# Attention, expert layer and second layer on one core: thresholds in pairs, v and the exchange at other steps

## Chip, cores, metric

One core of a Trainium2 chip. The time is the device time of one execution in microseconds (us). The engines are named as the profile names them: PE (TensorE, products), DVE (VectorE), ACT (ScalarE), POOL (GpSimd), SP (SyncE, which here issues nearly all DMAs).

## What is computed

Attention with a threshold near each row's maximum, then a layer of eight experts of which each token uses one, then a second layer. All inputs are 32-bit floats; the change touches the attention alone.

```python
batch, n_heads, seq, head_dim = (4, 8, 576, 64)
def _attn_ref(q, k, v, tau):
    scale = 1.0 / np.sqrt(q.shape[-1])
    scores = scale * np.matmul(q, k.transpose(0, 1, 3, 2))
    thresh = np.max(scores, axis=-1, keepdims=True) - tau
    scores = np.where(scores >= thresh, scores, -1000000000.0)
    scores = scores - np.max(scores, axis=-1, keepdims=True)
    attn = np.exp(scores)
    attn = attn / (np.sum(attn, axis=-1, keepdims=True) + 1e-09)
    return np.matmul(attn, v)

def reference(q, k, v, tau, moe_*, moe2_*):
    attn_out = _attn_ref(q, k, v, tau)
    x = attn_out.transpose(0, 2, 1, 3).reshape(B * S, H * D)
    x = _moe_ref(x=x, **moe)      # 2304 tokens, one of 8 experts each
    return _moe2_ref(x=x, **moe2) # (h - tanh(h)) @ w_out
```

## The kernel before

The attention runs as 16 units, numbered 0 to 15; a unit is one head of two batch entries. A unit has nine steps, t = 0 to 8, of 128 query rows against 576 keys, so that there are 144 steps in one row, numbered i = 9u + t. Whatever else a unit needs (loads, splitting and transposing q and k, the exchange, the weights of v, P times V, logits) is put at a step relative to the unit's first one, and at a phase 0 to 3 of that step, by the table `PL`; `PFIRST` and `PLAST` override it for the first and the last unit. `run` walks through the steps and issues: phase 0, the scores of step i+2 on PE, phase 1, the maximum of step i+1 on DVE (`smax`, L234) and its exponential on ACT (`sexp`, L240), the mask of step i on DVE (`smask`, L253, which multiplies the exponential by "score at or above the threshold" and sums the row), the threshold of step i+1 on DVE (`sthr`, L244), then phases 2 and 3. That order is the order in which each engine executes: every engine and SP's queue work strictly in order, and the waits between them are semaphores that the framework derives from who writes and reads what.

Score tiles lie in PSUM in three buffers of two banks each (`asp`), so the scores of step i+2 need the buffer that the mask of step i-1 frees. One more bank, tile `ops`, holds in disjoint columns two halves of P times V (`self.ops`, products L297, read by `pv_out`, L303), the logits (`self.lm`, products L557, read at L564 and L566) and the v sums (`self.vsum`, product L130, read at L135). The last bank, tag "t", is a single buffer through which pass the transposes of q and k (`tr`, L167), the exchange products (`turn`, L204) and the transposes for the logits (L549).

The exchange of a unit makes a copy of q with its two halves of partitions swapped: three products with a flip matrix (`s0`, `s1`, `s2`, L204), each copied out by DVE (`x0`, `x1`, `x2`, L209). After it come the transposes of k in two parts (`k0`, `k5`, L167), each copied out by ACT (`ek0`, `ek5`, L193). They are placed five to seven steps ahead of the unit that needs them, that is in steps t = 2 to 5 of the unit before.

v is loaded for four units at a time by six DMAs from SP (`lv`, L106 and L108). Each of the four units has a maximum of |v| on DVE (`vm`, L126), then once for the four a sum on PE (`vn`) and three small operations on DVE (`vc`, L135 to L137) make a scale. The first four units have places of their own in `PFIRST`; the others, beginning at units 4, 8 and 12, take theirs from `PL`. The weights after the mask go through a cast on ACT (L261), a subtraction on POOL (L265) and a DMA transpose that SP issues (`te`, L272), three per unit, each for three of its P times V groups, seven steps later.

All that follows the attention (experts, second layer) stays as it is.

Of the kernel before, what the change touches and what calls it, by code (L numbers as in the profile page):

```python
# [11 lines left out]
F32 = mybir.dt.float32  # L12
# [6 lines left out]
ALU = mybir.AluOpType  # L19
# [11 lines left out]
class Attn:  # L31
# [3 lines left out]
    def __init__(self, tc, ctx, q, k, v, tau, xtok, ident):  # L35
        self.tc, self.nc = tc, tc.nc
        self.q, self.k, self.v = q, k, v
        self.xtok, self.ident = xtok, ident
        nc = self.nc
        e = ctx.enter_context  # L40
        self.one = e(tc.tile_pool(name="a1", bufs=1))
        self.ld = e(tc.tile_pool(name="ald", bufs=2))
        self.wk = e(tc.tile_pool(name="awk", bufs=2))
        self.sp = e(tc.tile_pool(name="asp", bufs=3, space=PSUM))
        self.tp = e(tc.tile_pool(name="atp", bufs=1, space=PSUM))
        one = self.one
        self.raw, self.x2, self.vv, self.vs, self.vh, self.ka = {}, {}, {}, {}, {}, {}
        self.X, self.rr, self.rqk, self.tpu = {}, {}, {}, {}
        w = one.tile([128, 1], F32, name="warm")
        nc.vector.memset(w, 0.0)  # L50
        nc.scalar.activation(out=w, in_=w, func=AF.Exp)
        t = one.tile([128, 1], F32, name="tau")
        nc.gpsimd.dma_start(out=t, in_=tau.to_broadcast([128, 1]))
        self.load_qk(0, 0, 0, 1, nc.sync)
        self.load_qk(0, 1, 0, 1, nc.scalar)
        self.identr = one.tile([128, 128], F32R, name="identr")
        nc.vector.tensor_copy(self.identr, ident)
        self.flip = one.tile([128, 128], F32R, name="flip")
        for o in (0, 64):
            nc.vector.tensor_copy(self.flip[:, o:o + 64], ident[:, 64 - o:128 - o])  # L60
        self.g8 = one.tile([128, 1], F32, name="g8")
        nc.vector.tensor_scalar(out=self.g8, in0=t, scalar1=0.0, scalar2=0.125, op0=ALU.is_ge, op1=ALU.mult)
        self.ntau = one.tile([128, 1], F32, name="ntau")
        nc.vector.tensor_scalar(out=self.ntau, in0=t, scalar1=0.0, scalar2=-1.0, op0=ALU.max, op1=ALU.mult)
        z = one.tile([128, 64], F32, name="z64")
        nc.gpsimd.memset(z, 0.0)
        self.QA, self.QB = [], []
        for i in range(2):
            for lst, nm in ((self.QA, "qa"), (self.QB, "qb")):
                tl = one.tile([128, 2 * QS], F32R, name=f"{nm}{i}")  # L70
                nc.vector.tensor_copy(tl[:, S:S + 64], z)
                lst.append(tl)
        bank = self.tp.tile([128, 512], F32, name="ops")
        self.ops = bank[:, 0:6 * D].rearrange("p (a b d) -> p a b d", a=2, b=3)
        w = 6 * D + 9 * H
        self.lm = bank[:, 6 * D:w].rearrange("p (t e) -> p t e", t=9)
        self.vsum = bank[:, w:w + 4]
        self.c14 = one.tile([128, 128], F32, name="c14")
        nc.gpsimd.memset(self.c14, 2.0 ** -14)
        self.em, self.e16, self.et, self.sums = {}, {}, {}, {}  # L80
# [147 lines left out]
                i += 1  # L228
        return ps

    def smax(self, ps):
        nc = self.nc
        n = self.wk.tile([128, 2], F32, tag="n", name="n", bufs=6)
        nc.vector.tensor_reduce(out=n[:, 0:1], in_=ps[:, :, 0:288], axis=AX.XY, op=ALU.max, negate=True)  # L234
        return n

# [3 lines left out]
        nc.scalar.activation(out=e, in_=ps[:, :, 0:288], func=AF.Exp, bias=n[:, 0:1])  # L240
        return e

    def sthr(self, n):
        self.nc.vector.tensor_scalar(out=n[:, 1:2], in0=n[:, 0:1], scalar1=-1.0, scalar2=self.ntau, op0=ALU.mult, op1=ALU.add)  # L244

    def smask(self, u, t, ps, n, e):
        nc = self.nc
# [58 lines left out]
    def store(self, u):  # L306
        nc = self.nc
        P, h = divmod(u, H)
        if h % 2 == 1:
            c = slice((h - 1) * D, (h + 1) * D)  # L310
            X = self.X[u // 2]
            for j in range(2):
# [4 lines left out]

    LD = (6,)

    PL = {"lq": (-21, 1), "lk": (-31, 2), "lv": (-12, 1), "hi0": (-16, 2), "hi1": (-15, 3), "lo0": (-13, 1),  # L320
# [15 lines left out]

    AFTER = ["lq hi0", "lk hi1", "hi0 lo0", "hi1 lo1", "lo0 q0", "lo0 q4", "lo0 m", "lo1 m", "lo1 k0", "lo1 k5", "q0 eq0",
             "eq0 m", "m em", "em q4", "q4 eq4", "eq4 k0", "k0 ek0", "ek0 k5", "k5 ek5", "eq0 swap", "em swap", "eq4 swap", "vm vn", "vn vc", "vc vw", "vw vh", "vh vl", "se sl", "sl te", "po2 st",
             "po0 t0", "po1 t1", "po2 t2", "t0 v0", "v0 t1", "t1 v1", "v1 t2", "t2 v2", "v0 l0", "v1 l1", "v2 l2", "l0 la", "l1 la", "l2 la", "de rc", "em s0", "eq4 s0", "s0 x0", "x0 s1", "s1 x1", "x1 s2", "s2 x2"]

    def run(self, units, moe=None):
        nc = self.nc
        NU = len(units)
        sched = {}
        PL = self.PL
        for x in self.AFTER:
            x, y = x.split()
            assert PL[x] < PL[y] or PL[x] == PL[y] and list(PL).index(x) < list(PL).index(y), (x, y)

        def at(b, job, f, *a):  # L350
            i, ph = PL[job]
            sched.setdefault((b + i, ph), []).append((f, a))

        for n, u in enumerate(units):
            b = 9 * n
            PL = {**self.PL, **(self.PFIRST if n == 0 else self.PLAST if n == NU - 1 else {})}
            if n % 4 == 0:
# [46 lines left out]
        steps = [(u, t) for u in units for t in range(9)]  # L404
        ps, nn, ee = {}, {}, {}
        first, last = min(sched)[0], max(sched)[0]
        for i in range(first, last + 1):
            if i == 4 and moe:
                moe.consts()
            for f, a in sched.get((i, 0), []):  # L410
                f(*a)
            if 0 <= i + 2 < len(steps):
                ps[i + 2] = self.scores(*steps[i + 2])
            for f, a in sched.get((i, 1), []):
                f(*a)
            if 0 <= i + 1 < len(steps):
                nn[i + 1] = self.smax(ps[i + 1])
                ee[i + 1] = self.sexp(ps[i + 1], nn[i + 1])
            if 0 <= i < len(steps):
                self.smask(*steps[i], ps.pop(i), nn.pop(i), ee.pop(i))  # L420
            if 0 <= i + 1 < len(steps):
                self.sthr(nn[i + 1])
            for ph in (2, 3):
                for f, a in sched.get((i, ph), []):
                    f(*a)
# [933 lines left out]
```

## Time and profile before

| | us |
|---|---|
| timed runs: median (lowest, highest of 3) | 1076.59 (1075.49, 1080.34) |
| profiled execution | 1076.63 |
| its span, first to last instruction | 1074.5 |
| busy: PE / DVE / ACT / POOL | 957.3 / 895.3 / 671.5 / 730.7 |
| first maximum L234 to last mask L253, starts | 15.2 to 332.1 |

The profile is one execution. A row of an instruction gives its start from the span's start, its duration, engine, line, operation, output and input, and in brackets how long the engine sat idle before it and which instruction released it. Durations of neighbours on DVE overlap by some 0.08 us in this profile, so that costs are read from start to start. The attention fills the first third of the span.

### The profile page before, as it was taken

How to read it: one execution, taken by the hardware profiler on the slowest of the kernel's cores; microseconds unless marked ns; L12 is line 12 of the kernel's file. 1: busy time of each engine (PE TensorE's matmuls, PEld its weight loads, DVE VectorE, ACT ScalarE, POOL GpSimd, SP SyncE). 2: the span in 40 equal slices, each digit the busy share in tenths (PEclk: the TensorE clock that was granted, in tenths of full speed). 3: DMA queues.
4: the chain of work that ended last, by engine and by line, in shares of the span. 5: the costliest groups of instructions: out<-in, count | busy, mean ns of one | idle time of the engine just before them, and what ended most of it. 6: DMA issues, size and time to landing. Idle time of an engine off the chain costs nothing.

```text
span 1074.5 us, 20770 instructions
## 1 busy us (share of the span) xinstructions
PE 957.3 (89%) x7342; PEld 876.6 (82%) x7342; DVE 895.3 (83%) x1635; ACT 671.5 (62%) x1262; POOL 730.7 (68%) x645
## 2 busy tenths in 40 slices
PE   4688897887787488999999988999999999999997
PEld 3576786776677387989999988888999999998986
DVE  5899888888884698977798876998989889888894
ACT  5797887986974154444455557666665666656662
POOL 3897887886874364455656567787867768677763
PEclk9698888898988599999999999999999999999999
DMA  6798999998989485877787976220101101000000
GB/s 160 145 213 165 211 205 152 225 202 163 175 155 169 149 292 199 278 227 247 258 290 252 295 247 177 76 76 20 40 8 38 30 20 40 8 31 1 20 11 30
DMA packets 247368, 153.16 MB, mean 143 GB/s; under 512 B 179642, under 2 KB 222028, under 8 KB 247261
## 3 DMA queue, kind: packets, MB, share of 16 engines
q1 hardware_dynamic: 243501, 141.02, 53.2%
q0 software_dynamic: 3312, 10.49, 2.8%
q8 instruction: 59, 0.97, 0.4%
q14 instruction: 48, 0.39, 0.1%
q10 hardware_dynamic: 448, 0.30, 0.1%
HBM read 85.08 MB, written 23.60 MB: 101 GB/s over the span
## 4 chain that ended last, share of the span: by engine, by line
PE 50%; DVE 9%; issue 3%; DMA 2%; ACT 1%; POOL 0%; another core or an unknown queue 0%; POOLq 0%; DVEq 0%; SPq 0%; ACTq 0%
PE h L1040 25%; PE y L1123 15%; PE y L1095 9%; DVE w L1236 2%; DVE w L1237 2%; PE t L1017 1%; DVE w L1234 1%; DMA xr<-rows,idx 1%; DVE cv L1157 1%; DVE tm L1235 1%; DVE w L1238 1%; DMA raw<-in_moe_w_dram 1%; DVE w L1010 1%; DMA raw<-wscr 0%; DVE cm L1159 0%
## 5 line engine op out<-in xcount | busy, mean ns | idle before, releaser
L265 POOL TENSOR_TENSOR e<-em,e 128x1024 f16<-128x1024 f32 (+1 forms) x98 | 158.1, 1613 | 55.0 <-ACT e L261 23.5
L1233 POOL TENSOR_SCALAR tm<-u 128x384 uint8<-128x384 f32 x88 | 129.7, 1474 | 51.4 <-ACT u L1229 50.8
L1040 PE MATMUL h<-xa,w 128*128 128x256 f32 (+6 forms) x864 | 140.5, 313 | 7.6 <-DVE hbuf L1076 6.8
L1095 PE MATMUL y<-hbuf,w 128*128 128x256 f32 (+6 forms) x864 | 139.5, 310 | 0.6 <-ACT yo L1098 0.6
L1040 PEld LDWEIGHTS h<-xa,w 128*128 128x128 f32 x864 | 130.5, 194 | 9.9 <-DVE hbuf L1076 8.1
L240 ACT ACTIVATE e<-sps,n 128x576 f32<-128x576 f32 x144 | 110.6, 768 | 34.8 <-DVE n L234 33.7
L1010 POOL TENSOR_TENSOR w<-raw,w 128x1024 fp32r<-128x1024 f32 x36 | 91.8, 2551 | 56.0 <-ACT w L1008 28.8
L1095 PEld LDWEIGHTS y<-hbuf,w 128*128 128x128 f32 x864 | 127.5, 191 | 1.3 <-ACT yo L1098 0.8
L1236 DVE SCALAR_TENSOR_TENSOR w<-y,w 128x384 f32<-128x384 f32 x96 | 123.3, 1284 | 0.0
L1229 ACT ACTIVATE u<-h 128x384 f32<-128x384 f32 x96 | 47.1, 491 | 117.3 <-PE h L1040 116.4
L253 DVE SCALAR_TENSOR_TENSOR em<-sps,n,e 128x576 f32<-128x576 f32 x144 | 116.6, 810 | 4.0 <-ACT e L240 2.4
L234 DVE TENSOR_REDUCE n<-sps 128x1 f32<-128x576 f32 x144 | 107.1, 744 | 12.3 <-PE sps L226 11.8
L1250 POOL TENSOR_TENSOR gl<-w,gh 128x384 fp32r<-128x384 f32 x83 | 85.7, 1032 | 38.0 <-ACT gh L1249 38.0
L1040 PE MATMUL h<-xk,w 128*128 128x384 f32 x576 | 109.6, 338 | 0.7 <-DVE w L1010 0.5
L297 PE MATMUL ops<-vh,et 128*128 128x64 f16 (+1 forms) x2240 | 97.4, 201 | 13.0 <-DVE x L303 12.1
L1040 PEld LDWEIGHTS h<-xk,w 128*128 128x128 f32 x576 | 102.1, 188 | 5.6 <-DVE w L1010 1.3
L297 PEld LDWEIGHTS <-et 128*128 128x128 f16 (+1 forms) x2240 | 83.6, 107 | 25.3 <-issue 21.1
L261 ACT CAST e<-em 128x576 f16<-128x576 f32 x144 | 99.9, 695 | 1.2 <-DVE em L253 1.2
L1075 ACT ACTIVATE hbuf<-h 128x256 fp32r<-128x256 f32 (+6 forms) x72 | 31.2, 433 | 108.3 <-PE h L1040 108.2
L226 PE MATMUL sps<-ka,qa 128*128 128x288 f32 x320 | 87.7, 367 | 9.4 <-DVE em L253 5.7
L1008 ACT CAST w<-raw 128x1024 fp32r<-128x1024 f32 x72 | 75.6, 1051 | 21.4 <-DVE free L597 11.6
L1123 PE MATMUL y<-w,gh 128*128 128x512 f32 x258 | 81.1, 395 | 3.2 <-POOL w L1010 1.5
(228 smaller groups left out, 2296.8 us busy)
## 6 DMA issues: line engine op xcount, KB each, us to landing
raw<-in_moe_w_dram SPq DMA_DIRECT2D x64, 512.0 KB, 5.2
cv<-in_moe_w_in_dram SPq DMA_DIRECT2D x16, 512.0 KB, 5.0
cv<-in_moe_w_out_dram SPq DMA_DIRECT2D x16, 512.0 KB, 5.4
wscr<-cm SPq DMA_DIRECT2D x32, 256.0 KB, 3.2
raw<-wscr SPq DMA_DIRECT2D x16, 512.0 KB, 3.8
xw<-yT SPq DMA_DIRECT2D x24, 192.0 KB, 2.7
vv<-in_v_dram SPq DMA_DIRECT2D x8, 512.0 KB, 5.1
raw<-in_q_dram SPq DMA_DIRECT2D x6, 576.0 KB, 7.7
```

The lines of the kernel that those rows point to most:

```text
L234: nc.vector.tensor_reduce(out=n[:, 0:1], in_=ps[:, :, 0:288], axis=AX.XY, op=ALU.max, negate=True)
L240: nc.scalar.activation(out=e, in_=ps[:, :, 0:288], func=AF.Exp, bias=n[:, 0:1])
L253: nc.vector.scalar_tensor_tensor(out=self.em[u, g][:, i].rearrange("p (a b) -> p a b", a=2), in0=ps[:, :, 0:288], scalar=n[:, 1:2], in1=e, ...
L261: self.nc.scalar.copy(self.e16[u, g][:, i, 0:S], self.em[u, g][:, i])
L265: eng.tensor_tensor(out=e16[:, r, S + 64:], in0=em[:, r, 0:512], in1=e16[:, r, 0:512], op=ALU.subtract)
L297: nc.tensor.matmul(o[q], lhsT=et[:, base + c, q], rhs=vh[:, a, j, c if c < 5 else c - 5, :], start=(n == 0), stop=(n == len(terms) - 1))
L1010: (self.nc.gpsimd if pool else self.nc.vector).tensor_tensor(out=l, in0=raw, in1=h.bitcast(F32), op=ALU.subtract)
L1040: self.nc.tensor.matmul(out, lhsT=a, rhs=b, start=(i == 0), stop=(i == len(parts) - 1))
L1095: nc.tensor.matmul(self.ys[d], lhsT=a[:, f % 2, s], rhs=b, start=(f == 0 and i == 0), stop=(f == 7 and i == 2))
L1123: nc.tensor.matmul(self.ys[m], lhsT=a[:, s], rhs=b[:, f % 2], start=(f == 0 and i == 0), stop=(f == 15 and i == 2))
L1233: nc.gpsimd.tensor_scalar(out=mk, in0=u, scalar1=RCUT * RCUT, scalar2=None, op0=ALU.is_gt)
L1236: V.scalar_tensor_tensor(out=w, in0=y, scalar=b, in1=w, op0=ALU.add, op1=ALU.mult)
```

## The change

Three things are done at once. (1) `smax` puts the negated maxima of two neighbouring steps into one tile of four words (maximum, threshold, maximum, threshold), and in every even step, right behind the maximum of step i+1 and its exponential, one subtraction makes both thresholds of the pair from -tau, which now stands twice in PSUM (`ntau2`, two columns of the bank `ops`). Odd steps issue none. (2) v is loaded at step -18 of its group instead of -12, its maxima come at -5 instead of -7, its sum and scale at -1 instead of -3. (3) The exchange copies `x0`, `x1`, `x2` come one or two phases later, the first k transposes move from phase 0 to phase 1 (behind the scores), their copy on ACT from phase 0 to phase 2, and the second k transposes from phase 2 to phase 3.

```diff
         self.vsum = bank[:, w:w + 4]
+        self.ntau2 = bank[:, w + 4:w + 6]
+        nc.vector.tensor_copy(self.ntau2, self.ntau.to_broadcast([128, 2]))
...
-    def smax(self, ps):
+    def smax(self, ps, i):
         nc = self.nc
-        n = self.wk.tile([128, 2], F32, tag="n", name="n", bufs=6)
+        if i % 2 == 0:
+            self.n2 = self.wk.tile([128, 2, 2], F32, tag="n", name="n", bufs=4)
+        n = self.n2[:, i % 2]
...
-    def sthr(self, n):
-        self.nc.vector.tensor_scalar(out=n[:, 1:2], in0=n[:, 0:1], scalar1=-1.0, scalar2=self.ntau, op0=ALU.mult, op1=ALU.add)
+    def sthr(self):
+        n = self.n2
+        self.nc.vector.tensor_tensor(out=n[:, :, 1], in0=self.ntau2, in1=n[:, :, 0], op=ALU.subtract)
...
-    PL = {"lq": (-21, 1), "lk": (-31, 2), "lv": (-12, 1), "hi0": (-16, 2), "hi1": (-15, 3), "lo0": (-13, 1),
+    PL = {"lq": (-21, 1), "lk": (-31, 2), "lv": (-18, 1), "hi0": (-16, 2), "hi1": (-15, 3), "lo0": (-13, 1),
...
-          "eq4": (-8, 0), "k0": (-5, 0), "ek0": (-5, 0), "k5": (-5, 2), "ek5": (-4, 0), "swap": (-8, 0),
-          "s0": (-7, 2), "x0": (-7, 3), "s1": (-6, 1), "x1": (-6, 2), "s2": (-6, 3), "x2": (-6, 3),
-          "vm": (-7, 3), "vn": (-3, 1), "vc": (-3, 2), "vw": (4, 3), "vh": (5, 3), "vl": (6, 1),
+          "eq4": (-8, 0), "k0": (-5, 1), "ek0": (-5, 2), "k5": (-5, 3), "ek5": (-4, 0), "swap": (-8, 0),
+          "s0": (-7, 2), "x0": (-6, 0), "s1": (-6, 1), "x1": (-6, 3), "s2": (-6, 3), "x2": (-5, 0),
+          "vm": (-5, 3), "vn": (-1, 1), "vc": (-1, 2), "vw": (4, 3), "vh": (5, 3), "vl": (6, 1),
...
             if 0 <= i + 1 < len(steps):
-                nn[i + 1] = self.smax(ps[i + 1])
+                nn[i + 1] = self.smax(ps[i + 1], i + 1)
                 ee[i + 1] = self.sexp(ps[i + 1], nn[i + 1])
+                if i % 2 == 0:
+                    self.sthr()
             if 0 <= i < len(steps):
                 self.smask(*steps[i], ps.pop(i), nn.pop(i), ee.pop(i))
-            if 0 <= i + 1 < len(steps):
-                self.sthr(nn[i + 1])
```

The list of what must come after what (`AFTER`) gains "x2 k0".

## Rows read from the trace of the kernel before

**Rows 1.** Windows: us; busy (x count) PE, PEld, DVE, ACT, POOL; PEclk; DMA; GB/s

```profile
80.00:335.00 255.00, 211.47 (x2749) 189.53 (x2750) 222.16 (x575) 211.61 (x370) 207.22 (x212) 0.89 0.99 183
```

**Rows 2.** Waits of DVE, 15 to 335: who <- whom: us in total, times, longest

```profile
DVE n L234 <- PE sps L226: 11.8, 17, 3.2
DVE qb L209 <- PE tws L204: 9.4, 18, 0.8
DVE pm L126 <- DMA vv<-in_v_dram: 9.3, 3, 5.3
DVE em L253 <- ACT e L240: 2.4, 11, 0.5
```

**Rows 3.** Timeline of DVE, a step without waits (start, duration, instruction)

```profile
258.67 0.75 DVE L234 TENSOR_REDUCE n<-sps 128x1 f32<-128x576 f32 x1
259.33 0.81 DVE L253 SCALAR_TENSOR_TENSOR em<-sps,n,e 128x576 f32<-128x576 f32 x1
...
260.07 0.21 DVE L244 TENSOR_SCALAR n<-n,ntau 128x1 f32<-128x1 f32 x1
260.19 0.74 DVE L234 TENSOR_REDUCE n<-sps 128x1 f32<-128x576 f32 x1
```

**Rows 4.** Groups by line (busy us, mean ns | idle before); L135 with ns min/median/max

```profile
L1157 DVE SCALAR_TENSOR_TENSOR cv<-cv,cm 128x512 uint32<-128x512 uint32 x32 | 41.7, 1303 | 1.1
L1237 DVE SCALAR_TENSOR_TENSOR w<-y,w 128x384 f32<-128x384 f32 x96 | 74.8, 780 | 10.4 <-DVE w L1236 0.5
...
L135 DVE TENSOR_SCALAR pm<-ops x4: 151/154/163, 38.5 to 256.2; 128x4 f32<-128x4 f32 x4
```

**Rows 5.** Timeline, two engines on interleaved words of one tile (cv)

```profile
396.74 0.43 DVE L1159 TENSOR_SCALAR cm<-cv 128x512 f32<-128x512 f32 x1
396.74 0.69 ACT L1163 ACTIVATE cv<-cv 128x512 f32<-128x512 f32 x1 [1.04 <-DVE cv L1157]
```

**Rows 6.** Timeline, logits read beside products in the same bank

```profile
148.18 1.00 PE L557 MATMUL ops<-wg,xT 128*128 128x8 f32 x4
...
149.57 0.97 PE L297 MATMUL ops<-vh,et 128*128 128x64 f16 x14
150.57 0.23 DVE L566 TENSOR_TENSOR L<-L,ops 128x72 f32<-128x72 f32 x1 [0.82 <-PE ops L297]
```

**Rows 7.** Timeline of DVE and PE, eighth step (t = 7) of unit 13

```profile
292.46 0.76 DVE L234 TENSOR_REDUCE n<-sps 128x1 f32<-128x576 f32 x1
...
295.29 0.76 DVE L234 TENSOR_REDUCE n<-sps 128x1 f32<-128x576 f32 x1 [0.64 <-PE sps L226]
...
293.55 0.97 PE L297 MATMUL ops<-vh,et 128*64 128x64 f16 x28
```

**Rows 8.** Timeline of DVE, SP and PE around the third load of v; landings of transposes

```profile
245.16 0.82 DVE L126 TENSOR_REDUCE pm<-vv 128x1 f32<-128x640 f32 x1 [5.34 <-DMA vv<-in_v_dram]
...
236.62 0.63 SPq L106 DMA_DIRECT2D vv<-in_v_dram  x1
...
224.83 4.07 SPq L272 DMA_TRANSPOSE et<-e  x1
...
234.53 0.58 PE L297 MATMUL ops<-vh,et 128*128 128x64 f16 x14
...
DMA to landing us min/median/max: 5.9/6.9/9.0
```

**Rows 9.** Timeline of PE and ACT, fifth step (t = 4) of unit 10

```profile
225.59 0.53 PE L167 MATMUL tps<-identr,x 128*128 128x128 f32 x4 [0.45 <-DVE qb L209]
...
226.16 0.59 ACT L193 CAST ka<-tps 128x512 fp32r<-128x512 f32 x1 [0.90 <-PE tps L167]
...
226.65 0.75 ACT L240 ACTIVATE e<-sps,n 128x576 f32<-128x576 f32 x1
...
227.43 0.67 ACT L261 CAST e<-em 128x576 f16<-128x576 f32 x1
...
227.93 0.51 PE L226 MATMUL sps<-ka,qa 128*128 128x288 f32 x2
```

More of the change, by code (lines that the diff above doesn't have):

```diff
@@ L338 @@
              "eq0 m", "m em", "em q4", "q4 eq4", "eq4 k0", "k0 ek0", "ek0 k5", "k5 ek5", "eq0 swap", "em swap", "eq4 swap", "vm vn", "vn vc", "vc vw", "vw vh", "vh vl", "se sl", "sl te", "po2 st",
-             "po0 t0", "po1 t1", "po2 t2", "t0 v0", "v0 t1", "t1 v1", "v1 t2", "t2 v2", "v0 l0", "v1 l1", "v2 l2", "l0 la", "l1 la", "l2 la", "de rc", "em s0", "eq4 s0", "s0 x0", "x0 s1", "s1 x1", "x1 s2", "s2 x2"]
+             "po0 t0", "po1 t1", "po2 t2", "t0 v0", "v0 t1", "t1 v1", "v1 t2", "t2 v2", "v0 l0", "v1 l1", "v2 l2", "l0 la", "l1 la", "l2 la", "de rc", "em s0", "eq4 s0", "s0 x0", "x0 s1", "s1 x1", "x1 s2", "s2 x2", "x2 k0"]
     def run(self, units, moe=None):
```

## Prediction, made before the change was timed

> **What bounds the kernel now.** The change touches the attention stage alone, some 330 of the 1074.5 us, so I read the stage first and not the page. The windows view [rows 1] shows VectorE (DVE) busy for 222.2 of the 255.0 us from 80 to 335, against 211.6 for ScalarE (ACT), 211.5 for TensorE (PE) and 207.2 for GpSimd: DVE is the fullest engine, but the other three are close behind, so an operation taken from DVE is not sure to shorten anything. PE also ran at a mean of 0.89 of its clock there, a mixture of 2.4 and 1.2 GHz. The waits of DVE [rows 2] say where its other time went: 11.8 us for scores, 9.4 us for the exchange products `tws`, 9.3 us in three waits for the DMA of v, the longest 5.3 us, and 2.4 us for the exponential.
>
> Where nothing holds DVE, a step is [rows 3]: maximum from 258.67, mask from 259.33, threshold from 260.07, next maximum from 260.19, 1.52 us in all. An instruction starts some 0.08 us before the one ahead has ended as long as it doesn't need its result: the mask starts 0.66 after the maximum, the threshold 0.74 after the mask, and the threshold, 0.21 long, delays the next maximum by 0.12 to 0.13. That 0.125, and not 0.21, is what one threshold costs. The order of before also keeps one instruction between each result and its reader.
>
> **A. One subtraction for two thresholds.** It removes 144 thresholds and adds 72. An odd step then has maximum and mask alone, 1.40 us, a gain of 72 x 0.125 = 9.0 us. In an even step the subtraction stands between the maximum it reads and the mask that reads it, and DVE has to wait for its own result twice. Two rows show what that costs [rows 4]: L1157, which reads what the instruction ahead wrote, has 1.1 us of idle time over 32, 34 ns each; L1237, which waits for DVE and for another engine as the mask does, has 10.4 us over 96, 108 ns each. The nearest row to the subtraction itself is L135, 4 elements out of PSUM in 154 ns. So an even step is 0.75 for the full maximum + 0.034 to 0.108 + 0.154 + 0.108 + 0.74 for the mask = 1.79 to 1.86, against 1.52: the 72 of them lose 19 to 24 us. Net, where DVE sets the pace throughout: +10 to +15 us. The cover is what DVE now waits for anyway, right behind the subtraction: the 2.4 us for exponentials goes; of the exchange waits, those in the third step of the six even units from 4 to 14 fall in an even step and take 0.3 each, 2 us; of the 11.8 us for scores, 8.6 come beside the longest, 3.2 at the start, and I let about half of them, 4 us, hide it. That leaves 12 - 8.5 = **+3.5 us**; the ends are -9 (every even step hidden) and +15 (none).
>
> The two maxima of a pair lie interleaved with their thresholds in one tile, and the exponential reads a maximum while the subtraction writes beside it. If that counted as a conflict each pair would wait for an exponential. The trace speaks against it [rows 5]: L1159 on DVE read the odd words of a tile from 396.74 on while L1163 on ACT wrote the even words of the same tile from 396.74 on.
>
> **B. tau in the PSUM bank of the products.** `ntau2` lies in the bank into which the P times V products (L297), the logits and the v sums are written. Such neighbours exclude each other [rows 6]: L566 reads the logits columns, whose last product L557 ended at 149.18, DVE was free at 149.76, yet it began only at 150.57, 0.82 later, when an L297 product into other columns of that bank had ended. So each subtraction waits for the P times V products issued before it, and those after it wait for the subtraction. Queued behind the waiting subtraction on DVE are the mask, and behind that the PSUM buffer that the next scores need. The price is read at the worst place, the eighth step of odd units [rows 7]: the maximum ended at 293.22, the products at 294.52, 1.30 later. The mask would then start at 294.52 + 0.04 + 0.154 + 0.108 = 294.82 and the next maximum at 295.56 instead of 295.29, since 0.64 of waiting for scores followed anyway: 0.27 net. There are seven odd units with such a step, 1.9 us; elsewhere the products mostly end just before the maximum, for which I add 1 us. B = **+3 us**; the ends are 0 and 7 x 1.30 = 9 us.
>
> The Trainium skill has a rule that speaks against this placement: "PSUM — Partial Sum Buffer", section "PSUM bank collisions raise a hardware error", says that two engines may not be in one bank (and quadrant of partitions) at the same time even at different addresses, so that software guards by bank and not by address. The 0.82 us of L566 agree with it; guarded by address alone, B would be nothing and the sum 3 us lower.
>
> **C. v loaded six steps earlier, its maximum two steps later.** The maximum of v (L126) [rows 8] waited 5.34 us for the load that SyncE (SP) issued from 236.62 on; the three such waits sum to 9.3 us [rows 2], and DVE, in order, held everything behind them. Six steps earlier the load lands over 10 us ahead: -9.3 us. Two things come back. First, the maxima no longer stand between the second exchange copy and the third, so three units get the waits for products that the others have, 9.4 us in 18 or 0.5 each [rows 2]: +1.5. Second, SP's queue is in order, and the six issues of v, at 0.63 and a little more each, 4.0 us, move in front of two transposes, the first issued at 224.83, and of four stores of X that nobody in the stage reads. The first transpose's product started at 234.53, 9.7 us after the issue, of which landing takes 5.9 to 9.0 (median 6.9): a slack of 0.7 to 3.8. Shifted by 4.0, it comes 0.2 to 3.3 us late, 1.2 at the median, of which I put down 1 us. The other two groups' transposes are issued somewhat longer ahead, and I take them to hold. C = -9.3 + 1.5 + 1 = **-7 us**, ends -9.3 and 0 (all three groups late by 2 to 3 us). One v sum and its three small DVE operations keep their distance from the maxima: nothing.
>
> **D. The exchange.** On DVE the three copies `x0` to `x2` keep their order among its instructions, because nothing of DVE's stands between the old place and the new: nothing. On PE the first k transposes (`k0`) go behind the scores, so the scores are no longer behind the 0.45 that `k0` waits for `x2` [rows 9]; 15 units x 0.45 = 6.8 us is the most this can give back. But on ACT their copy goes behind the exponential and the cast: 226.16 + 0.75 + 0.67 + 0.59 = 228.2 instead of 226.75. `k5` uses the same single PSUM tile and waits for that copy, and behind `k5` on PE are the next scores: 228.2 + 0.5 = 228.7 instead of 227.93, 0.8 late. Twelve units without v maxima (which cover it) x 0.8 = 9 us at most. DVE is slower by about 0.3 in the even step there, so a part is covered: **+3 us**, ends -7 and +9.
>
> **The sum.** 3.5 + 3 - 7 + 3 = +2.5 us of span; the copy that fills `ntau2` runs once before the first scores and counts nothing. The profiled execution took 1076.63 us, the median of the three timed runs is 1076.59, so the forecast is 1076.6 + 2.5 = 1079.1 us. A measurement of this kernel tells about 0.5%, 5.4 us, from no change.
>
> **The rivals.** (1) *The paired threshold is paid in full.* The place is the even step; the price is the two waits of DVE for itself, +12 to +15 instead of +3.5, with B at 3, C at -7 and D at +3: 1088 to 1091, on average 1089. For it: DVE is the fullest engine, and the waits for scores move with DVE, because a score tile starts when a mask frees its buffer. Against it: 2.4 + 9.4 + 11.8 us of waiting right behind. It turns the result slower than 1082 as soon as A costs over 6.4, that is, when less than half of the 12 is hidden. (2) *Only the v wait counts.* A and D vanish in existing waits, B nearly so: -9.3 + 1.5 + 0.5 gives 1069. For it: the 5.34 us are plain and lie on the fullest engine; against it: the gaps of [rows 4] and the bank of [rows 6]. (3) *The wait moves from v to the transposes.* SP's 4.0 us make the products late in all three groups, C goes to -1: 1085. For it: the 0.7 us of slack at the slowest landing; against it: the longer lead of the other two groups. (4) *The pair waits for the exponential after all*, 0.75 us [rows 9] x 72 = 54 more: 1133; against it, [rows 5].
>
> **How the numbers follow.** Forecast 0.39; (1) 0.20; (2) 0.27; (3) 0.13; (4) 0.01. Slower by over 0.5% are (1), (3) and (4), 0.34; faster (2), 0.27; same the forecast, 0.39. The likeliest is the forecast, 1079.1 us, by itself 1073 to 1082. Cases of either sign hold most of the chance, so the range takes in (2) with a little more of v's wait, 1067, and (1) to its end, 1091.
>
> **What would show it.** A: a pair of steps of 3.15 to 3.25 us against 3.05, with a gap ahead of the subtraction and of the mask. B: waits of the new subtraction for L297, about one per odd unit, near 1 us. C: no wait of L126 for the DMA; waits of L297 for a transpose near the end of units 2, 6 and 10. D: waits of the maximum for scores in the sixth and seventh step of most units. I am wrong if the subtraction costs far less than 0.3 us in its step, if the k copies on ACT don't hold PE up, or if the mask's wait for the exponential is what DVE's new gaps fall into everywhere.

## The result, and the profile after

| | us, median (lowest, highest) | runs | ratio to before [95%] |
|---|---|---|---|
| before, timed beside it | 1076.05 | 4 | 1 |
| changed | 1083.92 (1082.18, 1085.51) | 4 | 1.0067 [1.004, 1.0094] |

The change makes the kernel 7.2 us slower (0.0067 x 1076.05), a little beyond the 0.5% that can be told from no change. The time lies inside the range of the forecast, 1067 to 1091, but the forecast itself, 1079.1, was 4.8 us too low and on the other side of the 0.5%. Rival (3), 1085, came nearer. The profiled execution took 1085.51 us, its span is 1083.5 us.

The span grew by 9.0 us, and 6.3 of them lie between the first and the last mask (313.7 before, 320.0 after); the first mask starts 1.0 later. The windows view from the first mask to the last, in the kernel before and in the changed one (us; busy and count of PE, PEld, DVE, ACT, POOL, then PEclk, DMA, GB/s):

```profile
18.43:332.13 313.70, 256.31 (x3222) 227.83 (x3221) 276.76 (x723) 260.85 (x454) 254.32 (x294) 0.88 0.95 179
```

```profile
19.41:339.40 319.99, 259.75 (x3208) 228.68 (x3207) 274.07 (x649) 263.78 (x453) 254.25 (x294) 0.90 0.93 174
```

DVE has 2.7 us less work there, and TensorE's granted clock is not lower (0.90 against 0.88). The kernel became slower all the same, because DVE's idle time rose from 36.9 to 45.9 us. DVE's waits from 15 to 345 us, which takes in the longer stage, to be laid beside [rows 2] (in this kernel the maximum is L238, the exponential L244, the subtraction L249, the mask L258, the exchange copy L211, the products of P and V L302):

```profile
DVE n L238 <- PE sps L228: 17.7, 23, 3.9
DVE qb L211 <- PE tws L206: 8.2, 17, 0.9
DVE n L249 <- PE ops L302: 4.4, 6, 1.2
DVE em L258 <- ACT e L244: 3.1, 4, 1.8
```

The 9.3 us for v are gone, as foretold. In their place stand 5.9 more for scores and 4.4 for the products in the bank of `ntau2`; and the waits for exponentials, which the new gaps should have swallowed, are 3.1 in four, up to 1.8 each, where there were eleven of 0.5 at most. These four rows sum to 33.4 us, those of [rows 2] to 32.9, so they don't hold the 9.0 us of new idle time. The groups by line do (busy, mean ns, then all idle time just before them and the longer waits in it); first the mask before, then the mask and the subtraction after:

```profile
L253 DVE SCALAR_TENSOR_TENSOR em<-sps,n,e 128x576 f32<-128x576 f32 x144 | 116.6, 810 | 4.0 <-ACT e L240 2.4 <-issue 1.1 <-POOL x L122 0.3
```

```profile
L258 DVE SCALAR_TENSOR_TENSOR em<-sps,n,e 128x576 f32<-128x576 f32 x144 | 117.1, 813 | 11.9 <-ACT e L244 3.1 <-DVE n L249 0.5 <-ACT vv L142 0.5
...
L249 DVE TENSOR_TENSOR n<-ops,n 128x2 f32<-128x2 f32 x72 | 11.5, 160 | 10.4 <-PE ops L302 4.4
```

Take these waits off, and 0.2 us of short gaps are left before and 7.8 + 6.0 = 13.8 after. So the stretch changed by 13.6 of gaps, -2.7 of work and -4.6 for all waits taken together, which makes its 6.3 us. A pair of steps shows the gaps, in the timeline of DVE:

```profile
236.18 0.76 DVE L238 TENSOR_REDUCE n<-sps 128x1 f32<-128x576 f32 x1 [0.19 <-PE sps L228]
237.04 0.16 DVE L249 TENSOR_TENSOR n<-ops,n 128x2 f32<-128x2 f32 x1
237.33 0.82 DVE L258 SCALAR_TENSOR_TENSOR em<-sps,n,e 128x576 f32<-128x576 f32 x1
...
238.07 0.75 DVE L238 TENSOR_REDUCE n<-sps 128x1 f32<-128x576 f32 x1
...
239.48 0.75 DVE L238 TENSOR_REDUCE n<-sps 128x1 f32<-128x576 f32 x1
```

From maximum to maximum the even step takes 1.89 and the odd one 1.41; the even steps without a wait take 1.73 to 1.90, with 1.87 in the middle. The maximum ends at 236.94 and the subtraction starts at 237.04, that ends at 237.20 and the mask starts at 237.33: two gaps, 0.10 and 0.13 (0.10 in most steps), that [rows 4] had priced at 0.034 to 0.108.

### The profile page after: what moved, and what is told of

Its sections match the earlier page's. It is cut to its first block, busy times and chain, and to the rows that moved or that the text cites. A ratio compares the mean times of both kernels' runs of the same rounds, so it can differ in the third digit from the quotient of the medians.

```text
span 1083.5 us, 20711 instructions
## 1 busy us (share of the span) xinstructions
PE 962.9 (89%) x7342; PEld 879.9 (81%) x7342; DVE 892.1 (82%) x1564; ACT 675.0 (62%) x1262; POOL 731.4 (68%) x645
## 4 chain that ended last, share of the span: by engine, by line
PE 46%; DVE 11%; issue 3%; DMA 2%; ACT 2%; POOL 0%; another core or an unknown queue 0%; SPq 0%; POOLq 0%; DVEq 0%; ACTq 0%
PE h L1045 23%; PE y L1128 14%; PE y L1100 8%; DVE w L1242 2%; DVE w L1241 2%; DMA raw<-in_moe_w_dram 1%; DVE w L1239 1%; DVE cv L1162 1%; PE t L1022 1%; DVE w L1015 1%; DVE tm L1240 1%; DMA xr<-rows,idx 1%; ACT w L1013 1%; DVE w L1243 1%; DVE cm L1164 0%
## 5 line engine op out<-in xcount | busy, mean ns | idle before, releaser
L244 ACT ACTIVATE e<-sps,n 128x576 f32<-128x576 f32 x144 | 107.7, 748 | 46.9 <-DVE n L238 42.2
L258 DVE SCALAR_TENSOR_TENSOR em<-sps,n,e 128x576 f32<-128x576 f32 x144 | 117.1, 813 | 11.9 <-ACT e L244 3.1
L238 DVE TENSOR_REDUCE n<-sps 128x1 f32<-128x576 f32 x144 | 107.4, 746 | 17.8 <-PE sps L228 17.7
L1241 DVE SCALAR_TENSOR_TENSOR w<-y,w 128x384 f32<-128x384 f32 x96 | 121.7, 1268 | 0.0
L302 PEld LDWEIGHTS <-et 128*128 128x128 f16 (+1 forms) x2240 | 87.3, 108 | 29.5 <-issue 23.2
L302 PE MATMUL ops<-vh,et 128*128 128x64 f16 (+1 forms) x2240 | 97.4, 202 | 14.7 <-DVE x L308 7.6
L266 ACT CAST e<-em 128x576 f16<-128x576 f32 x144 | 96.6, 672 | 5.8 <-DMA et<-e 4.6
L1242 DVE SCALAR_TENSOR_TENSOR w<-y,w 128x384 f32<-128x384 f32 x96 | 79.5, 828 | 10.0
```

What stands on the lines that cost most here:

```text
L258: nc.vector.scalar_tensor_tensor(out=self.em[u, g][:, i].rearrange("p (a b) -> p a b", a=2), in0=ps[:, :, 0:288], scalar=n[:, 1:2], in1=e, ...
L302: nc.tensor.matmul(o[q], lhsT=et[:, base + c, q], rhs=vh[:, a, j, c if c < 5 else c - 5, :], start=(n == 0), stop=(n == len(terms) - 1))
L1241: V.scalar_tensor_tensor(out=w, in0=y, scalar=b, in1=w, op0=ALU.add, op1=ALU.mult)
L1242: V.scalar_tensor_tensor(out=w, in0=z, scalar=d, in1=w, op0=ALU.add, op1=ALU.mult)
```

## The experiments

Every kernel is the one before with some edit, or the changed one with an edit undone, timed in five rounds against the kernel before on the same chip. "Stretch" is first to last mask in the profiled execution (313.7 before, 320.0 changed). The kernels were timed on three chips, on which the kernel before took 1077.3, 1080.1 and 1077.7 us, so that kernels are compared by their ratios; in brackets is the 95% interval.

| kernel | edit | median us | ratio [95%] | stretch |
|---|---|---|---|---|
| e1_v | v part alone | 1077.87 | 1.0009 [0.9991, 1.0027] | 313.6 |
| e2_pairs | paired thresholds alone | 1081.36 | 1.0039 [1.0023, 1.0056] | 315.7 |
| e3_exch | exchange part alone | 1081.36 | 1.0047 [1.0029, 1.0066] | 318.0 |
| e4_pairs_sbuf | e2, tau in SBUF | 1104.34 | 1.0253 [1.0232, 1.0274] | |
| e11_pairs_ts | pairs by one scalar operation | 1104.27 | 1.0227 [1.0198, 1.0257] | |
| e5_vmax | only the later maxima of v | 1072.59 | 0.9934 [0.9912, 0.9957] | 307.0 |
| e8_vearly | only v loaded at -38 | 1069.94 | 0.9914 [0.9885, 0.9942] | 304.8 |
| e12_vearly_late | both | 1064.37 | 0.9882 [0.9858, 0.9907] | 302.5 |
| e10_exch_act | exchange, first k copy ahead of the exponential | 1082.34 | 1.0027 [1.001, 1.0044] | 317.6 |
| e14_vearly_exch | e8 and e10 | 1071.62 | 0.9937 [0.9916, 0.9959] | 310.4 |
| e6_pairs_v | changed, exchange part undone | 1081.68 | 1.0037 [1.002, 1.0055] | 317.1 |
| e13_after_vearly | changed, v loaded at -38 | 1082.46 | 1.004 [1.0025, 1.0055] | 317.1 |

### v alone

```diff
-          "lv": (-12, 1)
+          "lv": (-18, 1)
...
-          "vm": (-7, 3), "vn": (-3, 1), "vc": (-3, 2)
+          "vm": (-5, 3), "vn": (-1, 1), "vc": (-1, 2)
```

> Only the v part of the change: load at -18, maximum at -5, sum and scale at -1. Theory (the prediction's terms): the three waits of the v maximum for the DMA, 9.3 us in the profile before, go to 0; three exchange waits of about 0.5 us come in their place and late transposes cost some 1 us: 7 us faster than before, 1069. Rival, the wait moves to the transposes: 1 us faster at most.

It gained nothing (+0.09%). The 9.3 us for v are gone from DVE's waits, but others have come. Of e1_v, first the waits of DVE and of ACT from 15 to 335, then the timeline of SP, ACT and DVE around the third load:

```profile
DVE em L253 <- ACT e L240: 11.2, 13, 3.7
```

```profile
ACT e L261 <- DMA et<-e: 9.3, 4, 4.1
```

```profile
229.62 10.47 SPq L272 DMA_TRANSPOSE et<-e  x2
...
238.03 0.67 ACT L261 CAST e<-em 128x576 f16<-128x576 f32 x1 [4.09 <-DMA et<-e]
...
239.18 0.73 ACT L240 ACTIVATE e<-sps,n 128x576 f32<-128x576 f32 x1
...
240.01 0.82 DVE L253 SCALAR_TENSOR_TENSOR em<-sps,n,e 128x576 f32<-128x576 f32 x1 [3.70 <-ACT e L240]
```

The chain is plain, and it is not the one I had drawn. The transpose behind v's six issues is issued at 229.62 instead of 224.83 [rows 8]. What waits for it first is not a product on PE but the cast L261 on ACT: it writes into the buffer that this transpose reads (three buffers, the transpose is three groups old). The cast stands still for 4.09 us, behind it on ACT stand a copy of q and the exponential, and for the exponential the mask waits 3.70. It happens behind every one of the three loads: 1.78, 3.12 and 4.09 us on ACT, 9.0 of the row's 9.3. Before, that cast had no time to spare either; in the timeline of ACT of the kernel before it is the row

```profile
233.00 0.67 ACT L261 CAST e<-em 128x576 f16<-128x576 f32 x1
```

8.17 us behind the issue at 224.83 [rows 8], where in e1_v it came 8.41 behind the issue and waited. Asked for this one transpose alone (225 to 228 us), the DMA view of the kernel before gives its time from issue to landing:

```profile
et<-e SPq DMA_TRANSPOSE x1, 8.1
```

The cast started 0.1 us after it.

### Only the maxima later, or only the load far earlier

```diff
-          "vm": (-7, 3), "vn": (-3, 1), "vc": (-3, 2)
+          "vm": (-5, 3), "vn": (-1, 1), "vc": (-1, 2)
```

> The load of v where it was before (step -12); only its maximum, sum and scale two steps later. This tells the load's place on SP from the maxima. Theory, formed on e1_v: the earlier load pushes transposes behind it and their products stop PE in the last step of units 2, 6 and 10, which took back what the waits of the maximum gave. Then here no such stop appears, the maximum waits at most 1 to 2 us for its load, and the time is 6 to 8 us below before. Rival, the later maxima themselves cost what the wait gave: within 2 us of before.

```diff
-          "lv": (-12, 1)
+          "lv": (-38, 2)
...
-bufs=2) for x in ("pm", "sc")
+bufs=3) for x in ("pm", "sc")
```

> The load of v at step -38, where SP's queue had an idle stretch in the profile before (a third buffer for the two small tiles pm and sc goes with it); maxima where they were before. Theory: no wait of the maximum for the DMA, no late transposes: 8 to 9 us below before. Rival, any place of these six issues delays some transpose: within 2 us of before.

Both times came out: -7.1 us (0.0066 x 1080.1) and -9.3 us. In e5_vmax 0.5 us are left of the wait for v, in e8_vearly nothing. The reason that the first theory gives is not the one that e1_v shows: there no product waits for a transpose, the cast does. So moving the reader two steps took v's wait away by itself, and the load six steps earlier, put in front of those transposes, took the gain back: 0.9934 against 1.0009 with intervals apart. Late transposes are not gone altogether: ACT's cast waits 3.6 us for them in e5_vmax (3.1 of it behind the third load, at its old place) and 1.3 in e8_vearly.

> The kernel before with v loaded at step -38 phase 2 (three buffers for pm and sc) and with the later maxima of v as well. Theory: with v there in time, the place of the maxima is worth next to nothing, since they are equally long at either place: within 2 us of v loaded at -38 alone, 8 to 10 us below before. Rival: the maxima cover some waits for scores or for the exchange at one of the two places; then it differs from it by 3 us or more.

With both edits it came out 12.7 us below before (0.0118 x 1077.72), 3 us beyond e8_vearly; the two intervals overlap, so the theory is not refuted and the rival not shown. It is the fastest kernel of the study, below both. The granted clock of the stretch rose in these three kernels as well (0.89, 0.91 and 0.92 against 0.88), but DVE's waits for PE did not fall with it: for scores 12.5 us in e12_vearly_late against 11.8 before, for exchange products 9.8 against 9.4. What went is the wait for v.

### The pairs alone, and tau in SBUF

e2_pairs is the changed kernel with the v and exchange parts undone.

> Only the paired thresholds with tau in PSUM, everything else as before. Theory: a pair of steps takes 3.25 us where DVE sets the pace, against 3.05, and the subtraction waits for P times V products in the eighth step of odd units: with half of it covered 6.5 us slower than before, with none of it covered 15 us and more. Rival, the pair hides in existing waits: within 2 us of before.

It was 4.2 us slower: the half-covered case, a little cheaper. Its DVE waits:

```profile
DVE n L238 <- PE sps L228: 8.2, 9, 3.2
DVE pm L128 <- DMA vv<-in_v_dram: 7.9, 3, 5.4
DVE n L249 <- PE ops L302: 7.1, 11, 1.1
DVE qb L211 <- PE tws L206: 5.8, 12, 0.9
DVE em L258 <- ACT e L244: 0.3, 1, 0.3
```

Against [rows 2], the gaps were covered by 2.1 of the exponentials' 2.4, by 3.6 of the exchange products' 9.4, by 3.6 of the scores' 11.8, and by 1.4 of v's; the bank took 7.1. Seven of the eleven waits for the bank lie in the sixth step of odd units (0.30 to 0.58 us), four in the eighth (0.94 to 1.12). Next, the bank taken away by putting `ntau2` elsewhere:

```diff
-        self.ntau2 = bank[:, w + 4:w + 6]
+        self.ntau2 = one.tile([128, 2], F32, name="ntau2")
```

> The paired thresholds alone as in e2_pairs, but with the two copies of -tau in SBUF instead of the PSUM bank of the products. Theory: the gaps of 0.1 us ahead of the subtraction and of the mask stay, the waits for the products go: 2 to 3 us faster than e2_pairs. Rival, a subtraction with both inputs in SBUF is held up by GpSimd's operations (durations well over its 0.16 us): slower than e2_pairs.

The rival held, and by far: 23 us slower than e2_pairs. One line's durations (ns, min/median/max) of e4_pairs_sbuf, and its timeline of DVE and POOL:

```profile
L249 DVE TENSOR_TENSOR n<-ntau,n x72: 160/769/1976, 19.2 to 356.2; 128x2 f32<-128x2 f32 x72
```

```profile
218.00 2.14 POOL L270 TENSOR_TENSOR e<-em,e 128x1024 f16<-128x1024 f32 x1 [1.76 <-issue]
...
219.39 0.77 DVE L249 TENSOR_TENSOR n<-ntau,n 128x2 f32<-128x2 f32 x1
```

The subtraction of two elements ends here just as POOL's ends (220.16 and 220.14). It is so for all 44 of the 72 that took over 0.25 us: each ends within 0.03 us of the end of an operation of POOL. With one operand in PSUM (e2_pairs) the same line took 160 ns each time, though an operation of POOL ran all through 48 of the 72. The Trainium skill says so in "SBUF — State Buffer", section "Who interferes with whom": a DVE instruction with two SBUF inputs competes with a GpSimd instruction that reads SBUF, one with a single SBUF input outside the two-port modes does not. These rows agree. A scalar operation with a single tensor operand was to avoid both the bank and POOL:

```diff
+        self.nc.vector.tensor_scalar(out=n[:, :, 1], in0=n[:, :, 0], scalar1=-1.0, scalar2=self.ntau, op0=ALU.mult, op1=ALU.add)
```

> The paired thresholds as in e2_pairs, but made from the maxima by one scalar operation of the old kind on two elements, -tau in SBUF, so that nothing reads the bank of the products. Theory: 7.1 us of waits of the subtraction for products go, the gaps of 0.1 us stay, the operation is 0.05 us longer (3.6 us in all): 0 to 3 us faster than e2_pairs, still 1 to 4 us slower than before. Rival, the gaps cost nothing and the bank everything: as fast as before or faster.

A plain miss: by the ratios it is some 20 us slower than e2_pairs (0.0188 x 1080.1). Here 47 of the 72 took over 0.25 us, and again each ends within 0.04 us of the end of an operation of POOL. The line's durations in e11_pairs_ts, and those of the same operation on one element in the kernel before:

```profile
L247 DVE TENSOR_SCALAR n<-n,ntau x72: 228/722/1982, 19.7 to 358.0; 128x2 f32<-128x2 f32 x72
```

```profile
L244 DVE TENSOR_SCALAR n<-n,ntau x144: 202/209/216, 16.0 to 329.8; 128x1 f32<-128x1 f32 x144
```

So tau in PSUM is what makes the pairing bearable here, and what B costs by itself could not be measured.

### The exchange

```diff
-          "k0": (-5, 0), "ek0": (-5, 0), "k5": (-5, 2)
+          "k0": (-5, 1), "ek0": (-5, 2), "k5": (-5, 3)
...
-          "x0": (-7, 3), "s1": (-6, 1), "x1": (-6, 2), "s2": (-6, 3), "x2": (-6, 3)
+          "x0": (-6, 0), "s1": (-6, 1), "x1": (-6, 3), "s2": (-6, 3), "x2": (-5, 0)
```

> Only the exchange and the k transposes moved as in the change. Theory: the k copies on ACT come behind the exponential and the cast, the next scores start some 0.8 us later in the sixth step of most units, part of it covered: 3 us slower than before (0 to 9). Rival, the scores gain from standing ahead of the k transposes: 2 to 6 us faster.

5.1 us slower. DVE's waits for scores, 11.8 us before [rows 2], are in e3_exch

```profile
DVE n L234 <- PE sps L226: 21.2, 28, 3.5
```

The waits of PE for the tile through which the k transposes pass, in the kernel before, in e3_exch and in the changed kernel:

```profile
PE tps L167 <- DVE qb L209: 7.0, 15, 0.6
```

```profile
PE tps L167 <- ACT ka L193: 19.5, 15, 2.1
```

```profile
PE tps L169 <- ACT ka L195: 17.4, 15, 1.8
```

The 7.0 us that the first k transposes used to wait are given back but for one wait of 3.6 us in the first unit (3.4 in the changed kernel). The second ones now wait for the copy in all 15 units, 1.2 to 1.3 us on average. What lies behind such a wait, in the changed kernel's timeline of PE and DVE, steps t = 4 to 6 of unit 9:

```profile
214.10 0.75 PE L169 MATMUL tps<-identr,x 128*128 128x128 f32 x4 [1.67 <-ACT ka L195]
214.65 0.81 PE L228 MATMUL sps<-ka,qa 128*128 128x288 f32 x2
...
215.97 0.76 DVE L238 TENSOR_REDUCE n<-sps 128x1 f32<-128x576 f32 x1 [0.96 <-PE sps L228]
...
217.13 0.83 PE L228 MATMUL sps<-ka,qa 128*128 128x288 f32 x2
...
218.48 0.76 DVE L238 TENSOR_REDUCE n<-sps 128x1 f32<-128x576 f32 x1 [1.02 <-PE sps L228]
...
220.46 0.16 DVE L249 TENSOR_TENSOR n<-ops,n 128x2 f32<-128x2 f32 x1 [1.23 <-PE ops L302]
```

After 1.67 us of waiting PE runs two score tiles, one after the other, at 0.81 and 0.83 for their first half, where [rows 9] has 0.51; both are late for DVE, which waits 0.96 and 1.02, and then 1.23 for the products in tau's bank, because they too are late. The windows view of this stretch:

```profile
214.10:219.00 4.90, 4.90 (x32) 4.49 (x32) 2.92 (x7) 4.68 (x8) 2.52 (x3) 0.50 1.06 189
```

The granted clock is at its lower level, 1.2 GHz, for both score tiles, 4.9 us; in unit 9 of the kernel before it was so for the first alone (0.50 over 2.55 us, then 0.95). But unit 9 is not the rule. Over the five us from the second k transposes on, the granted clock is 0.75 in the mean of the 15 units before and 0.74 in the changed kernel (0.70 in e3_exch): lower in some units, higher in others. What the clock does to the price of such a wait shows in e3_exch, where the second k transposes of units 8 and 10 wait equally long, 1.04 us. Their windows of five us, and the next maximum in each:

```profile
194.80:199.80 5.00, 5.00 (x58) 4.53 (x59) 3.98 (x13) 4.93 (x9) 3.22 (x4) 0.66 1.04 201
233.68:238.68 5.00, 4.88 (x79) 4.51 (x80) 4.50 (x14) 5.00 (x9) 3.23 (x4) 1.00 1.07 210
```

```profile
196.37 0.76 DVE L234 TENSOR_REDUCE n<-sps 128x1 f32<-128x576 f32 x1 [0.74 <-PE sps L226]
...
234.85 0.76 DVE L234 TENSOR_REDUCE n<-sps 128x1 f32<-128x576 f32 x1 [0.34 <-PE sps L226]
```

In unit 8, at 0.66, the two maxima after that wait as well, 0.28 and 0.24; in unit 10, at 1.00, none does. Units 4 and 6 make the same pair (0.67, 0.28 and 0.29 at 0.66; 0.35 at 1.00). So the same wait of PE costs DVE some 1.25 us where the clock was at its lower level for a good part of the five us, and 0.35 where it was not. What lowered the clock in one unit and not in the other was not tried.

e10_exch_act has the same edit, but with the first copy left ahead of the exponential ("ek0" at (-5, 1)) and "k5" at (-5, 2).

> The exchange as in e3_exch, but the copy of the first k transposes on ACT stays ahead of the exponential (phase 1) and the second k transposes stay in phase 2. Theory: the loss of e3_exch, 4 us, is the late copy on ACT, which holds the second k transposes and behind them the scores: here the waits of the maximum for scores fall back to about 12 us and the time is within 2 us of before. Rival, the loss is the k transposes standing behind the scores: 3 to 5 us slower as e3_exch.

It landed between the two, 2.9 us above before. PE's wait for the copy fell as it should, and the waits for scores with it, but DVE's for v rose, and so did all waits of the mask, from 3.8 us before to 8.6; rows of its waits of PE and of DVE:

```profile
PE tps L167 <- ACT ka L193: 6.1, 9, 0.7
```

```profile
DVE pm L126 <- DMA vv<-in_v_dram: 12.5, 3, 5.4
...
DVE n L234 <- PE sps L226: 7.5, 6, 3.8
```

In e3_exch the row for v was 5.1 in three. So a part of what one gains or loses in the steps ahead of v's maximum seems to be set off in the wait for v.

> The kernel before with v loaded at step -38 phase 2 (three buffers for pm and sc) and with the exchange copies and k transposes of the change, except that the first k copy stays ahead of the exponential on ScalarE (phase 1) and the second k transposes at phase 2. Theory: with v's waits gone, what is left is the 4 us of waits for scores that this order took away: 2 to 4 us below v at -38 alone, 11 to 13 us below before. Rival: the exponential behind the copy is late for the mask, some 8 us of waits for it instead of 2, which eat that up: the same as v at -38 alone, or up to 3 us above it.

With v out of the way the good order of the exchange should have shown its 4 us. It showed none; it came out 6.8 us below before, 2.5 above e8_vearly, with intervals that overlap. The rival's time is right, and so is the wait that it names, but not what it puts ahead of the exponential. The waits of the mask for the exponential are 3.1 us in the row that names it, and more of them stand in a row without a name ("issue"):

```profile
DVE em L253 <- issue: 8.1, 10, 3.9
```

```profile
ACT e L261 <- DMA et<-e: 5.7, 2, 3.5
```

```profile
209.67 0.67 ACT L261 CAST e<-em 128x576 f16<-128x576 f32 x1 [3.46 <-DMA et<-e]
...
211.44 0.74 ACT L240 ACTIVATE e<-sps,n 128x576 f32<-128x576 f32 x1
...
212.27 0.82 DVE L253 SCALAR_TENSOR_TENSOR em<-sps,n,e 128x576 f32<-128x576 f32 x1 [3.87 <-issue]
```

The mask starts when the exponential is done, and this is late because the same cast is late for the same kind of transpose: 3.46 us here, in unit 9, and 2.20 in unit 5, where the mask waits 2.61. These two waits are 6.5 of the 8.1 us. Why the transposes are late there stays open.

### The changed kernel with one part undone

> The changed kernel with the exchange and the k transposes put back to the places of before: pairs and v alone. If the parts add up (v alone +0.09%, pairs alone +0.39%), it is 5 us slower than before, 2 us better than the whole change. Rival: the waits for scores that the late k copies make fall into gaps that the pairs open anyway, so that putting them back brings nothing: about 7 us slower than before, as the whole change.

+4.0 us (0.0037 x 1077.72): the sum of the parts, a little less. But the parts don't add up by being independent. With the exchange undone (first fence, e6_pairs_v) ACT's wait of the cast for the transposes is as long as in e1_v; in the changed kernel (second fence) it is half of that:

```profile
ACT e L266 <- DMA et<-e: 9.5, 4, 4.0
```

```profile
ACT e L266 <- DMA et<-e: 4.6, 4, 2.0
```

The steps of the changed kernel are the slower ones. My reading is that the stalls of the exchange lie between the transpose's issue and that cast and give it time, so that undoing one brings the other out.

```diff
-          "lv": (-18, 1)
+          "lv": (-38, 2)
...
-bufs=2) for x in ("pm", "sc")
+bufs=3) for x in ("pm", "sc")
```

> The whole change, but v loaded at step -38 phase 2 (three buffers for pm and sc) instead of -18 phase 1. Theory: what the change lost on v is the transposes behind its six issues; with these out of the way the mask's waits for the exponential at the eighth and ninth step of units 2, 6 and 10 go, and it is some 9 to 10 us faster than the whole change, 2 to 4 us below before. Rival: the waits of the paired subtraction and of the late k copies take up half of that, so that it stays 1 to 3 us above before.

+4.3 us, with an interval of 2.7 to 5.9: the theory fails, and the rival's end of 3 us is just inside. DVE's waits of e13_after_vearly:

```profile
DVE n L238 <- PE sps L228: 17.7, 21, 3.1
...
DVE n L249 <- PE ops L302: 4.8, 8, 1.0
```

The 3.1 us of waits for exponentials are gone but for 0.2, and the stretch is 2.9 us shorter, no more. In the changed kernel the late transposes cost only that; the rest of the 7.2 us, and of the 9.3 that were to be gained, is in the other two rows and in the gaps of A. Beside e12_vearly_late, which has v at the same places and neither pairs nor exchange, the stretch is 14.6 us longer (317.1 against 302.5). That is what A, B and D together cost when no wait for v hides any of it; I had put down 3.5 + 3 + 3 = 9.5. Nearly all of it is in A's gaps: the short gaps ahead of mask and subtraction are 13.6 us in e13_after_vearly (8.5 + 10.9 of idle time, less 5.8 of longer waits) and nothing in e12_vearly_late, DVE has 1.0 us less work, and the waits taken together are only 2.0 longer.

## Why the prediction was right or wrong

**A** was right in its working. The steps are 1.41 and 1.87 (1.40 and 1.79 to 1.86), the gaps less the work that went cost 13.6 - 2.7 = 10.9 us where I had 12 uncovered, the exponentials' waits vanished in e2_pairs, and about a third of the scores' and the exchange's waits (3.6 us of each) hid a part of the rest, where I had allowed 4 and 2. No row of e2_pairs or of the changed kernel has the subtraction waiting for ACT: rival (4) is out. What failed is the cover in the whole change: the waits for scores, 4 us of which were to hide it, rose by 5.9.

**B** was right in its place and reason, but it was put low: six waits of 0.19 to 1.23 us in the changed kernel, all in the eighth step of odd units, 4.4 us together, and 7.1 in e2_pairs, where I had 3 net and 9 at the end. No run tells B's price from A's. A and B together cost 4.2 us alone; with the 1.4 that v's wait gave up for them, 5.6, against 6.5.

**C** failed in its mechanism: alone it gave +0.09% instead of -7 us. The step is "The first transpose's product started at 234.53, 9.7 us after the issue", and with it "The other two groups' transposes are issued somewhat longer ahead, and I take them to hold". I asked who reads what the transpose writes, and not who writes what it reads. The cast that reuses its input stands 1.5 us earlier than the product (8.17 and 9.7 after the issue) and on an engine with the exponential behind it; all three groups were late. That is rival (3) in size and in the number of groups, by another wait than it named, and with 8.1 us from issue to landing of this very transpose the trace of before could have told it. In the whole change the late cast costs less, 2.9 to 3.1 us, so that C there comes to about 9.3 - 3.1 = 6.2 us gained: near what I had written, but by luck. My reading is that the change slows the steps in between. Rival (3), which lets the transposes cost 6 us more, came near the measured time by luck too.

**D** failed in size: "DVE is slower by about 0.3 in the even step there, so a part is covered: +3 us". Little was covered. The wait of the second k transposes is 1.2 us on average in 15 units, not 0.8 in twelve, and DVE's waits for scores rose by 9.4 us in e3_exch. How much of such a wait reaches DVE goes with the granted clock behind it, 0.35 or 1.25 us in the units compared above, and I had no term for it. Alone D cost 5.1 us while v's wait fell by 4.2 (9.3 to 5.1), together 9.3: the end of my range, not its value.

With these values the sum is 5.6 - 6.2 + 9.3 = 8.7 us against 7.2 measured; the prediction had 6.5 - 7 + 3 = 2.5. By this split the miss is D's. The split is one of several possible ones, since the terms hide one another: with the exchange at its old places the changed kernel gains 3.2 us (e6_pairs_v), just what I had written for D. The parts alone come to 0.09 + 0.39 + 0.47 = 0.95%, the whole to 0.67%; undoing the exchange's part, or loading v at -38, recovers some 3 us each, with intervals that overlap that of the whole change. DVE's account of the stretch hangs on no split: the gaps and the work came out as foretold, within about 1 us, and the waits fell by 4.6 us, where my terms let them fall by 9.5 (8.5 of cover and 7 of C, less 3 each for B and D). That, and not the price of A, put the forecast too low.

## What to carry to other kernels

Before a DMA is moved in front of others, look for both of the transfers' dependents: the reader of what they write, and the writer that reuses what they read; the earlier one sets the slack. When a wait is for a load, moving the reader may be free where moving the load is not. Terms that lie in the same few steps are not to be summed from single effects: a removed wait had been hiding others, and its removal brings out their full price. And a table of waits is not all idle time: here it summed to the same before and after, and the loss stood in gaps of a tenth of a microsecond, 13.6 us of them.

## What was not expected of the hardware

That an operation of DVE on two elements per partition could take 2 us. On two SBUF operands it took 160 to 1976 ns (median 769), as a scalar operation on two elements 228 to 1982 (722), in all cases of over 0.25 us up to the end of an operation of POOL; on one element 202 to 216, and with an operand in PSUM 159 to 161. The Trainium skill, in "SBUF — State Buffer", section "Who interferes with whom", puts scalar operations that enter a two-port mode under the same rule; that one element escapes and two don't is what these rows add.

Also, a dependent neighbour on DVE costs more than the instruction: the 160 ns of the subtraction come with gaps of 0.10 us each in most steps, where independent neighbours overlap by 0.08 [rows 3].
